# Retention, routed experts and a channel mix in one kernel: where the last two row blocks of wv are narrowed

## The chip, the cores and the metric

One core of a Trainium2 chip runs the whole program. The metric is the device time of one execution in microseconds (us). Before the change the median of three runs is 459.07 us.

## The reference, cut to what matters

Three layers follow one another on 2 x 768 tokens of width 512:

```python
x = retention(q, k, v, lam)                   # 8 heads of 64, blocks of 64
e = expert_of_each_token(x, w_gate, w_local)  # one expert of 8, in order of the sequence
y = p[e] * (relu(x @ w1[e]) @ w2[e])          # w1: 512 x 1024, w2: 1024 x 512
x_prev = shift(y, 1)
xk = mu_k * y + (1 - mu_k) * x_prev
xr = mu_r * y + (1 - mu_r) * x_prev
k = relu(xk @ w_k)                            # w_k: 512 x 1024
out = sigmoid(xr @ w_r) * ((k * k) @ w_v)     # w_r: 512 x 512, w_v: 1024 x 512
```

The last layer is the channel mix. Its three weights w_k, w_v and w_r are float64 and reach the kernel as 64-bit words, so they have to be turned into float32 ("narrowed") on the chip.

## The kernel before, in words

Every product is made in three matmuls of a rounded format (fp32r): each operand is split into a high part (a cast on ScalarE, ACT) and a low part (source minus high, on VectorE, DVE), and high x high, high x low and low x high are summed in PSUM (`split3`, L652, and `k_high` and `k_low` in the mix). Each engine works through its instructions in the order in which the program writes them.

*The experts* run one after another (`up`, L659, and `down`, L699), 256 token slots each. `up` makes four pieces of the hidden layer; for each, PE runs 24 matmuls into a PSUM tile `ps_h` (three such tiles), ACT writes the high part `hh` (L669) and DVE the low part `hl` (L670), after which the PSUM tile is free for the piece after the next two. `down` uses the four pieces in order. Within `up` and `down` the function `side_w` is called 8 times an expert, 64 times in all, counted here from 0. A call splits one or two staged weight pieces (`w_split`: cast L155, subtraction L156, and on the SP queue the load of the piece four further on) and takes `ns` steps of the narrowing.

*The narrowing* (`narrow`, L754) takes one 128 x 512 part in three steps of DVE work: `narrow_1` (L743, L744), `narrow_2` (L747, L748) and `narrow_3` (L751, L752). ACT has the magnitude of the next part (L739) at the end of the third step; the load of the part after the next (L767, 512 KB) is issued there too. The parts are 8 of wk, 4 of wr and 8 of wv. The first 18 are written back to DRAM by the SP queue (L788) and later loaded and split like any other weight. The last two, row blocks 6 and 7 of wv, aren't written: `divide` (L795) makes their two parts of `w2` at once. That makes 60 steps behind a first one that only loads. From call 4 to call 51 a call takes one step, and two where its number leaves 5 when divided by 8 (calls 5, 13, 21, 29, 37, 45); calls 52 to 54 take two each, and `divide` comes in calls 57 and 59.

*The channel mix* takes six groups of 256 tokens. The order of the program is k_begin and k_part for group 0, r_part 0, k_part 1, mix(1, 1), and then in turn v_part of one group, r_part of the next and k_part of the one after. `k_part` (L1042) makes four pieces; for each PE runs its matmuls into `ps_k`, ACT applies Relu into `rl` (L1064) and Square into `kh` (L1065), DVE makes `sq = rl * rl` (L1067) and the low part (L1068), and then `after(fp)` runs whatever is put there. For group 0 that is `first_k`: mix_first behind piece 0, `weigh(1)` (ACT, L995) behind piece 1, and behind piece 3 the transposes of group 1 (`fetch`), `mix(1, 0)` (DVE L906 and L915, ACT L902 and L914) and a read. `k_part` 1 needs `mix(1, 0)`. `v_part` (L1083) takes the eight row blocks of wv in order, three matmuls each (L655 to L657): high, low, high part of the block's weights.

Of the kernel before, what the change touches and what calls it, by code (L numbers as in the profile page):

```python
# [10 lines left out]
F32 = mybir.dt.float32  # L11
# [3 lines left out]
I32 = mybir.dt.int32  # L15
AF = mybir.ActivationFunctionType
ALU = mybir.AluOpType
# [4 lines left out]
P = 128  # L22
B, H, S, D = 2, 8, 768, 64
DM = H * D
NE, FF = 8, 1024
# [5 lines left out]
NF = FF // P  # L31
# [13 lines left out]
def kernel(  # L45
# [16 lines left out]
    act, dve, pool, pe, sp = nc.scalar, nc.vector, nc.gpsimd, nc.tensor, nc.sync  # L62
# [48 lines left out]
    NV = NF - 2  # L111
    wk32 = dp.tile([P, ND, FF], F32, name="wk32")
    wr32 = dp.tile([P, ND, DM], F32, name="wr32")
    wv32 = dp.tile([P, NV, DM], F32, name="wv32")
# [8 lines left out]
    W = {}  # L123
# [20 lines left out]
    def w_split(k=1, eng=dve):  # L144
        for _ in range(k):
            if at[1] >= len(pieces):
                return
            while at[0] <= at[1]:
                w_load()
            kind, i, src, n, f, j, m = pieces[at[1]]  # L150
            if (kind, i) not in W:
                W[kind, i] = w_tiles(kind, i, n, f)
            hi, lo = W[kind, i]
            t = staged.pop(at[1])
            act.copy(out=hi[:, j : j + m, :], in_=t)  # L155
            eng.tensor_tensor(out=lo[:, j : j + m, :], in0=t, in1=hi[:, j : j + m, :].bitcast(F32), op=ALU.subtract)  # L156
            at[1] += 1
            w_load()
# [21 lines left out]
    with ExitStack() as actx:  # L180
# [54 lines left out]
        for h in range(H):  # L235
            dve.tensor_tensor_scan(
                out=msk[:, h % 2, h // 2, :], data0=lams[:, h : h + 1].to_broadcast([P, P]), data1=ident, initial=0.0, op0=ALU.mult, op1=ALU.add
# [395 lines left out]
    with ExitStack() as bctx:  # L633
# [87 lines left out]
        ys, written = [], []  # L721
# [9 lines left out]
        def words(raw):  # L731
            return (
                raw.bitcast(mybir.dt.uint32).rearrange("p (n t) -> p n t", t=2)[:, :, 0],
                raw.bitcast(I32).rearrange("p (n t) -> p n t", t=2)[:, :, 1],
                raw.bitcast(F32).rearrange("p (n t) -> p n t", t=2)[:, :, 1],
            )

        def magnitude(raw, t):
            act.activation(out=t.bitcast(F32), in_=words(raw)[2], func=AF.Abs)  # L739

        def narrow_1(t):

            dve.tensor_scalar(out=t.bitcast(F32), in0=t.bitcast(F32), scalar1=2.0**-15, scalar2=TOP64, op0=ALU.max, op1=ALU.min)  # L743
            dve.tensor_scalar(out=t, in0=t, scalar1=3, scalar2=0x3FFFFFFF, op0=ALU.logical_shift_left, op1=ALU.bitwise_and)  # L744

        def narrow_2(raw, t, t2, p2):
            dve.scalar_tensor_tensor(out=t2, in0=words(raw)[1], scalar=-(1 << 30), in1=t, op0=ALU.bitwise_and, op1=ALU.bitwise_or)  # L747
            dve.tensor_scalar(out=p2, in0=t2, scalar1=-(1 << 23), scalar2=None, op0=ALU.bitwise_and)  # L748

        def narrow_3(raw, p2, low, t2, x):  # L750
            dve.scalar_tensor_tensor(out=low, in0=words(raw)[0], scalar=2.0**-52, in1=p2, op0=ALU.mult, op1=ALU.mult)  # L751
            dve.tensor_tensor(out=x, in0=low, in1=t2.bitcast(F32), op=ALU.add)  # L752

        def narrow():  # L754

            n = DM
            parts = []
            for src, dst in ((wk, wk32), (wr, wr32), (wv, wv32)):
                sv, dv = (x.rearrange("p a b -> p (a b)") for x in (src, dst))
                parts += [(sv[:, j : j + n], dv[:, j : j + n]) for j in range(0, dv.shape[1], n)]  # L760
            parts += [(wv[:, j, :], j) for j in range(NV, NF)]
            raws, ts = {}, {}

            def read(k):
                if k < len(parts):
                    raws[k] = bp.tile([P, n], mybir.dt.int64, name=f"raw64_{k}", tag="raw64")
                    sp.dma_start(out=raws[k], in_=parts[k][0])  # L767

            def begin(k):
                if k < len(parts):  # L770
                    ts[k] = tp.tile([P, n], I32, name="t1", tag="t1")
                    magnitude(raws[k], ts[k])

            read(0)
            read(1)
            yield
            begin(0)
            for k in range(len(parts)):
                t2 = tp.tile([P, n], I32, name="t2", tag="t2", bufs=3)
                narrow_1(ts[k])  # L780
                yield
                narrow_2(raws[k], ts[k], t2, ts[k])
                yield
                narrow_3(raws[k], ts[k].bitcast(F32), ts[k].bitcast(F32), t2, t2.bitcast(F32))
                if isinstance(parts[k][1], int):
                    whole.append((parts[k][1], t2.bitcast(F32)))
                else:
                    written.append(lambda t=t2, k=k: sp.dma_start(out=parts[k][1], in_=t.bitcast(F32)))  # L788
                begin(k + 1)
                read(k + 2)  # L790
                yield

        whole = []

        def divide():  # L795

            j, x = whole.pop(0)
            hi, lo = (w[:, j, :] for w in W["w2", NE])
            act.copy(out=hi, in_=x)
            dve.tensor_tensor(out=lo, in0=x, in1=hi.bitcast(F32), op=ALU.subtract)  # L800

        conv = narrow()
        perm = bp.tile([P, 2, 2 * P], F32R, name="perm", bufs=1)
# [128 lines left out]
        def side_w():  # L932
            c = calls[0]
            calls[0] += 1
            late = list(written)

            ws, ns, vs = 1, 1, 0
            if c < 4:
                ws, ns = (2, 2, 1, 1)[c], c == 2
            elif c >= 52:  # L940
                ws, ns, vs = ((1, 2, 0), (1, 2, 0), (1, 2, 0), (1, 0, 0), (1, 0, 0), (1, 0, 1), (1, 0, 0), (0, 0, 1), (1, 0, 0), (1, 0, 0), (0, 0, 0), (0, 0, 0))[c - 52]
            elif c % 8 == 5:
                ns = 2
            w_split(ws)
            for _ in range(ns):
                next(conv, None)
            for _ in range(vs):
                divide()
            for w in late:
                w()  # L950
            del written[: len(late)]
# [15 lines left out]
    with ExitStack() as mctx:  # L967
        mp = mctx.enter_context(tc.tile_pool(name="mp", bufs=2))
# [3 lines left out]
        GS = 2 * P  # L972
# [11 lines left out]
        def read(n):  # L984
            if n < NN:
                xgs[n] = xsp.tile([P, 2, DM], F32, name=f"xg{n}", tag="xs")
                for i in range(2):
                    u = unit(n, i)
                    sp.dma_start(out=xgs[n][:, i, :], in_=Y_n[u * P : (u + 1) * P, :])

        def weigh(n):
            if n < NN:
                for i in range(2):
                    u, x = unit(n, i), xgs[n][:, i, :]
                    act.activation(out=x, in_=x, func=AF.Copy, scale=pe_p[:, u : u + 1])  # L995
# [56 lines left out]
        def k_part(n, xk, pk, after):  # L1052

            k2[n] = []
            for fp in range(NF // 2):
                ds = (2, 3) if fp in pk else range(ND)
                if fp not in pk:
                    pk[fp] = psk.tile([P, 2, GS], F32, name=f"ps_k{n}{fp}", tag="k")
                ps = pk[fp]
                k_high(ps, fp, ds, xk)  # L1060
                k_low(ps, fp, ds, xk)
                rl = mp.tile([P, 2, GS], F32, name="rl", tag="rl")
                kh, kl = (mp.tile([P, 2, GS], F32R, name=f"k2{x}{n}{fp}", tag=f"k2{x}", bufs=NF) for x in "hl")
                act.activation(out=rl, in_=ps, func=AF.Relu)  # L1064
                act.activation(out=kh, in_=rl, func=AF.Square)  # L1065
                sq = mp.tile([P, 2, GS], F32, name="sq", tag="sq")
                dve.tensor_tensor(out=sq, in0=rl, in1=rl, op=ALU.mult)  # L1067
                dve.tensor_tensor(out=kl, in0=sq, in1=kh.bitcast(F32), op=ALU.subtract)  # L1068
                k2[n].append((kh, kl))
                after(fp)  # L1070

# [11 lines left out]
        def v_part(n, after):  # L1083
            b, g = todo[n]
            for t in range(2):
# [10 lines left out]
                    sp.dma_start(out=out[b, g * GS + t * P : g * GS + (t + 1) * P, w], in_=o[:, w])  # L1096
                after(t)

        def none(_):
            pass  # L1100

        def first_k(fp):
            if fp == 0:
                mix_first(1, 1)
                x_new(1)
                for a in range(2):
                    act.copy(out=xt[1][:, 2 * a : 2 * a + 2, 0:1], in_=px[1 + a][:, :, GS - 1 : GS])
            if fp == 1:
                weigh(1)
            if fp == NF // 2 - 1:  # L1110
                fetch(1)
                xk[1] = mix(1, 0)
                read(2)


        xk, xr = {0: x0[0]}, {}
# [2 lines left out]
        xr[0] = x0[1]  # L1119
        k_part(0, xk[0], pk, first_k)  # L1120
        r_part(0, xr[0])
        k_part(1, xk[1], {}, lambda fp: fp == 1 and weigh(2))
        xr[1] = mix(1, 1)
        for n in range(1, NN):

# [61 lines left out]
```

## Time and profile before

| what | value |
| --- | --- |
| runs of the kernel before | 459.07 us median (458.91, 459.07, 461.42) |
| the profiled execution's own time | 458.06 us |
| its span, first to last instruction | 456.4 us |
| PE busy | 436.7 us (96%) |
| DVE busy | 309.9 us (68%) |
| ACT busy | 229.2 us (50%) |
| mean granted TensorE clock | 0.993 |

The span runs from the first instruction to the last; some 1.7 us of the execution's time lie around it. Matmuls are pipelined, so PE's busy time says that PE had work in flight, not how much of its peak it gave. In the profile PE stands for TensorE's matmuls, DVE for VectorE, ACT for ScalarE, and SPq for the DMA queue of SyncE. An idle time in brackets is that of the engine just before the instruction, with what ended it.

### The profile page before, as it was taken

What the parts mean: (1) busy time and instruction counts of PE and PEld (TensorE: products, weight loads), DVE (VectorE), ACT (ScalarE), POOL (GpSimd) and SP (SyncE); (2) the same over time, 40 slices, a digit from 0 to 9 for tenths busy, and PEclk for the clock granted to TensorE, in tenths of its full rate; (3) what the DMA queues carried; (4) which work ended last, traced back from release to release, by engine and by line L of the source; (5) the groups of instructions that cost most, each with busy time, mean ns of one, the idle gap of its engine ahead of it and who ended that gap; (6) DMA issues with size and microseconds to landing.
All of it is one profiled execution on the core that took longest, in us unless ns stands there. A gap on an engine that the chain in (4) does not pass through costs nothing.

```text
span 456.4 us, 8308 instructions
## 1 busy us (share of the span) xinstructions
PE 436.7 (96%) x3243; PEld 391.3 (86%) x3243; DVE 309.9 (68%) x602; ACT 229.2 (50%) x386; POOL 65.6 (14%) x92
## 2 busy tenths in 40 slices
PE   6999988999798999999999999999999999999996
PEld 4888776979688898989898999998898988989886
DVE  6678875775989899998989995746255262552501
ACT  2455532565475465747465653866255462653410
POOL 3433323500312021232110101000000000000000
PEclk9999998999998999999999999999999999999999
DMA  7999934497979999999989741201102002010001
GB/s 254 341 382 341 412 124 139 147 315 259 323 244 324 322 312 355 293 366 302 335 303 311 242 144 43 93 1 34 60 1 92 1 25 68 0 47 1 12 36 47
DMA packets 29111, 85.03 MB, mean 186 GB/s; under 512 B 4351, under 2 KB 5131, under 8 KB 29068
## 3 DMA queue, kind: packets, MB, share of 16 engines
q1 hardware_dynamic: 25004, 73.45, 47.1%
q0 software_dynamic: 2624, 8.39, 5.1%
q10 hardware_dynamic: 1440, 2.62, 1.5%
q8 instruction: 26, 0.43, 0.4%
q14 instruction: 17, 0.14, 0.1%
HBM read 68.71 MB, written 15.74 MB: 185 GB/s over the span
## 4 chain that ended last, share of the span: by engine, by line
PE 69%; DVE 13%; DMA 8%; ACT 4%; issue 4%; POOL 1%; SPq 1%; DVEq 0%; ACTq 0%; POOLq 0%
PE ps_y L655 5%; PE ps_y L657 5%; PE ps_y L656 5%; PE ps_v L655 5%; PE ps_v L656 5%; PE ps_v L657 5%; PE ps_h L655 5%; PE ps_h L656 5%; PE ps_h L657 5%; PE ps_k L1028 4%; PE ps_k L1029 4%; PE ps_k L1035 4%; DMA raw<-in_w_dram 4%; DVE w1l L156 2%; PE ps_r L655 2%
## 5 line engine op out<-in xcount | busy, mean ns | idle before, releaser
L655 PE MATMUL ps_h<-xsTh,w1h 128*128 128x256 f32 x256 | 73.6, 288 | 4.4 <-DVE hl L670 4.4
L656 PE MATMUL ps_h<-xsTl,w1h 128*128 128x256 f32 x256 | 73.4, 287 | 0.1
L657 PE MATMUL ps_h<-xsTh,w1l 128*128 128x256 f32 x256 | 73.0, 285 | 0.0
L1067 DVE TENSOR_TENSOR sq<-rl 128x512 f32<-128x512 f32 x24 | 16.6, 692 | 56.3 <-ACT rl L1064 56.3
L655 PEld LDWEIGHTS ps_h<-xsTh,w1h 128*128 128x128 f32 x256 | 49.7, 194 | 5.4 <-DVE hl L670 4.8
L655 PE MATMUL ps_y<-w2h,hh 128*128 128x512 f32 (+1 forms) x136 | 52.6, 387 | 0.0
L657 PE MATMUL ps_y<-w2h,hl 128*128 128x512 f32 (+1 forms) x136 | 51.9, 382 | 0.0
L656 PE MATMUL ps_y<-w2l,hh 128*128 128x512 f32 (+1 forms) x136 | 51.9, 382 | 0.0
L656 PEld LDWEIGHTS ps_h<-xsTl,w1h 128*128 128x128 f32 x256 | 49.8, 195 | 0.9 <-DVE xsTl L174 0.5
L156 DVE TENSOR_TENSOR w1l<-raw,w1h 128x1024 fp32r<-128x1024 f32 x38 | 46.3, 1220 | 5.3 <-ACT w1h L155 4.9
L657 PEld LDWEIGHTS ps_h<-xsTh,w1l 128*128 128x128 f32 x256 | 49.8, 195 | 0.0
L156 DVE TENSOR_TENSOR w2l<-raw,w2h 128x1024 fp32r<-128x1024 f32 x35 | 42.6, 1216 | 3.7 <-ACT w2h L155 3.5
L739 ACT ACTIVATE t<-raw 128x512 f32<-128x512 f32 x20 | 13.5, 677 | 55.8 <-DMA raw<-in_wk_dram 24.4
L155 ACT CAST w1h<-raw 128x1024 fp32r<-128x1024 f32 x38 | 38.7, 1052 | 3.5 <-DMA raw<-in_w_dram 3.0
L155 ACT CAST w2h<-raw 128x1024 fp32r<-128x1024 f32 x35 | 36.7, 1048 | 6.0 <-DMA raw<-in_w_dram 4.9
L655 PE MATMUL ps_v<-w2h,k2h 128*128 128x512 f32 (+1 forms) x104 | 39.2, 377 | 0.0
L656 PE MATMUL ps_v<-w2l,k2h 128*128 128x512 f32 (+1 forms) x104 | 38.8, 373 | 0.0
L657 PE MATMUL ps_v<-w2h,k2l 128*128 128x512 f32 (+1 forms) x104 | 38.8, 373 | 0.0
L726 POOL DMA_INDIRECT Y_n<-y,sidx x16 | 17.9, 1118 | 144.1 <-ACT y L716 81.3
L657 PEld LDWEIGHTS ps_y<-w2h,hl 128*128 128x128 f32 x136 | 25.6, 188 | 5.5 <-DVE hl L670 0.2
L656 PEld LDWEIGHTS ps_y<-w2l,hh 128*128 128x128 f32 x136 | 25.6, 188 | 5.1
L655 PEld LDWEIGHTS ps_y<-w2h,hh 128*128 128x128 f32 x136 | 25.6, 188 | 5.1
(210 smaller groups left out, 964.4 us busy)
## 6 DMA issues: line engine op xcount, KB each, us to landing
raw<-in_w_dram SPq DMA_DIRECT2D x64, 512.0 KB
kv<-in_kv_dram SPq DMA_DIRECT2D x12, 512.0 KB
qk<-in_qk_dram SPq DMA_DIRECT2D x11, 512.0 KB
raw<-in_wk_dram SPq DMA_DIRECT2D x8, 512.0 KB
raw<-in_wv_dram SPq DMA_DIRECT2D x8, 512.0 KB
out_dram<-o SPq DMA_DIRECT2D x11, 256.0 KB
X_n<-xn ACTq DMA_DIRECT2D x10, 256.0 KB
xg<-Y_n SPq DMA_DIRECT2D x10, 256.0 KB
```

The source lines that it names most:

```text
L155: act.copy(out=hi[:, j : j + m, :], in_=t)
L156: eng.tensor_tensor(out=lo[:, j : j + m, :], in0=t, in1=hi[:, j : j + m, :].bitcast(F32), op=ALU.subtract)
L655: pe.matmul(ps, wh, xh, start=first, stop=False)
L656: pe.matmul(ps, wh, xl, start=False, stop=False)
L657: pe.matmul(ps, wl, xh, start=False, stop=last)
L726: pool.indirect_dma_start(out=Y_n[:, :], out_offset=bass.IndirectOffsetOnAxis(ap=sidx[:, t, e : e + 1], axis=0), in_=y, in_offset=None)
L739: act.activation(out=t.bitcast(F32), in_=words(raw)[2], func=AF.Abs)
L1028: pe.matmul(ps[:, j, :], wkh[:, d, f], x[0][:, d, :], start=j == d == 0, stop=False, skip_group_check=True)
L1029: pe.matmul(ps[:, j, :], wkl[:, d, f], x[0][:, d, :], start=False, stop=False, skip_group_check=True)
L1035: pe.matmul(ps[:, j, :], wkh[:, d, f], x[1][:, d, :], start=False, stop=d == ND - 1, skip_group_check=True)
L1067: dve.tensor_tensor(out=sq, in0=rl, in1=rl, op=ALU.mult)
```

## The change

The two row blocks leave the experts: `narrow` makes 18 parts, in the order wk, wv, wr, and every call from 4 to 51 takes one step; calls 52 to 54 still take two. `divide` goes. In the channel mix a new generator, `last_rows`, loads row block 6, narrows it, splits it, and then does the same for row block 7, in pieces placed by hand between the pieces of k_part 0 and k_part 1. Its tiles take the room of `sq`: the square is now made in place in `rl`.

```diff
-            for src, dst in ((wk, wk32), (wr, wr32), (wv, wv32)):
+            for src, dst in ((wk, wk32), (wv, wv32), (wr, wr32)):
...
-            parts += [(wv[:, j, :], j) for j in range(NV, NF)]
...
-            elif c % 8 == 5:
-                ns = 2
+                ws, ns = int(c not in (59, 62, 63)), 2 if c < 55 else 0
...
-                sq = mp.tile([P, 2, GS], F32, name="sq", tag="sq")
-                dve.tensor_tensor(out=sq, in0=rl, in1=rl, op=ALU.mult)
-                dve.tensor_tensor(out=kl, in0=sq, in1=kh.bitcast(F32), op=ALU.subtract)
+                dve.tensor_tensor(out=rl, in0=rl, in1=rl, op=ALU.mult)
+                dve.tensor_tensor(out=kl, in0=rl, in1=kh.bitcast(F32), op=ALU.subtract)
...
+        def last_rows():
+            def read(j):
+                raw = mp.tile([P, DM], mybir.dt.int64, name=f"r64_{j}", tag="r64", bufs=1)
+                sp.dma_start(out=raw, in_=wv[:, j, :])
+                return raw
+            raw = read(NV)
+            yield
+            for j in range(NV, NF):
+                t, t2 = (mp.tile([P, DM], I32, name=f"{x}c{j}", tag=f"{x}c", bufs=1) for x in ("t1", "t2"))
+                hi, lo = (w[:, j, :] for w in W["w2", NE])
+                magnitude(raw, t)
+                yield
+                narrow_1(t)
+                narrow_2(raw, t, t2, t)
+                yield
+                x = t2.bitcast(F32)
+                narrow_3(raw, t.bitcast(F32), t.bitcast(F32), t2, x)
+                if j + 1 < NF:
+                    raw = read(j + 1)
+                yield
+                act.copy(out=hi, in_=x)
+                dve.tensor_tensor(out=lo, in0=x, in1=hi.bitcast(F32), op=ALU.subtract)
+                yield
...
+            if fp in (1, 2):
+                next(rows)
             if fp == 1:
                 weigh(1)
...
         r_part(0, xr[0])
-        k_part(1, xk[1], {}, lambda fp: fp == 1 and weigh(2))
+        next(rows)
+        def second_k(fp):
+            if fp == 1:
+                weigh(2)
+            if fp != 1:
+                next(rows)
+        k_part(1, xk[1], {}, second_k)
+        next(rows)
+        next(rows)
         xr[1] = mix(1, 1)
```

So block 6 has its load at the start of the channel mix, its magnitude behind piece 1 of k_part 0, its first two steps behind piece 2, its third step behind r_part 0 and its split behind piece 0 of k_part 1. Block 7 has its load behind the third step of block 6, its magnitude behind piece 2 of k_part 1, its first two steps behind piece 3, and its third step and its split between k_part 1 and mix(1, 1).

## Rows read from the trace of the kernel before

**Rows 1.** Windows: length, busy time by engine, then granted clock, DMA share, GB/s.

```profile
114.80:117.30 2.50, 0.00 (x1) 0.00 (x0) 2.46 (x5) 0.93 (x2) 1.23 (x1) 1.00 0.99 324
...
141.10:143.10 2.00, 0.06 (x2) 0.01 (x1) 1.97 (x5) 0.00 (x0) 0.29 (x1) 1.00 0.93 352
...
144.00:147.40 3.40, 3.40 (x18) 3.40 (x17) 3.37 (x6) 3.25 (x5) 1.98 (x2) 0.50 0.92 322
...
299.40:442.00 142.60, 142.60 (x867) 128.11 (x868) 61.57 (x105) 66.63 (x122) 0.49 (x3) 1.00 0.09 30
```

**Rows 2.** Waits of PE from 100 to 160 us: total, times, longest.

```profile
PE ps_h L655 <- DVE hl L670: 4.4, 2, 2.5
```

**Rows 3.** Timeline of PE: k_part 1 waits, and block 7 in v_part 0.

```profile
299.39 0.39 PE L1028 MATMUL ps_k<-w1h,w1h 128*128 128x256 f32 x1 [0.52 <-ACT w1h L914]
...
315.06 0.39 PE L656 MATMUL ps_v<-w2l,k2h 128*128 128x512 f32 x1
```

**Rows 4.** Timeline of DVE in the first three experts: start, duration, instruction.

```profile
113.57 0.42 DVE L743 TENSOR_SCALAR t<-t 128x512 f32<-128x512 f32 x1
...
114.37 1.22 DVE L156 TENSOR_TENSOR w1l<-raw,w1h 128x1024 fp32r<-128x1024 f32 x1
115.50 0.68 DVE L747 SCALAR_TENSOR_TENSOR t<-raw,t 128x512 int32<-128x512 int32 x1
...
116.57 0.68 DVE L670 SCALAR_TENSOR_TENSOR hl<-ps_h,hh 128x512 fp32r<-128x512 f32 x1
...
142.35 0.68 DVE L670 SCALAR_TENSOR_TENSOR hl<-ps_h,hh 128x512 fp32r<-128x512 f32 x1
...
150.80 0.68 DVE L670 SCALAR_TENSOR_TENSOR hl<-ps_h,hh 128x512 fp32r<-128x512 f32 x1
```

**Rows 5.** Timeline of DVE: a third step, a `divide`, and the channel mix's start.

```profile
254.28 0.68 DVE L751 SCALAR_TENSOR_TENSOR t<-raw,t 128x512 f32<-128x512 uint32 x1
...
255.61 0.42 DVE L743 TENSOR_SCALAR t<-t 128x512 f32<-128x512 f32 x1
...
267.78 0.68 DVE L800 TENSOR_TENSOR w2l<-t,w2h 128x512 fp32r<-128x512 f32 x1
...
286.30 0.68 DVE L1067 TENSOR_TENSOR sq<-rl 128x512 f32<-128x512 f32 x1
287.09 0.69 DVE L1068 TENSOR_TENSOR k2l<-sq,k2h 128x512 fp32r<-128x512 f32 x1
287.70 0.87 DVE L906 SCALAR_TENSOR_TENSOR t<-ps_f,mus,t 128x256 f32<-128x256 f32 x2
...
295.63 0.89 DVE L906 SCALAR_TENSOR_TENSOR t<-xt,mus,t 128x256 f32<-128x256 f32 x2 [0.49 <-ACT t L902]
```

**Rows 6.** Timeline of PE: `down` of expert 2, first use of the fourth piece's `hl`.

```profile
153.10 0.40 PE L657 MATMUL ps_y<-w2h,hl 128*128 128x512 f32 x1
```

**Rows 7.** Timeline of ACT: in expert 1, and the channel mix's groups 0 and 1.

```profile
116.37 0.67 ACT L739 ACTIVATE t<-raw 128x512 f32<-128x512 f32 x1 [2.76 <-DMA raw<-in_wk_dram]
116.94 0.58 ACT L669 ACTIVATE hh<-ps_h 128x512 fp32r<-128x512 f32 x1
...
286.20 0.63 ACT L1065 ACTIVATE k2h<-rl 128x512 fp32r<-128x512 f32 x1
...
290.41 1.32 ACT L995 ACTIVATE xg<-xg,pe_p 128x512 f32<-128x512 f32 x2
291.64 0.57 ACT L1064 ACTIVATE rl<-ps_k 128x512 f32<-128x512 f32 x1
...
310.24 0.60 ACT L1064 ACTIVATE rl<-ps_k 128x512 f32<-128x512 f32 x1 [1.62 <-PE ps_k L1035]
```

**Rows 8.** The ACT cast of a `divide`, in the timeline of ACT.

```profile
266.27 0.62 ACT L799 CAST w2h<-t 128x512 fp32r<-128x512 f32 x1
```

**Rows 9.** Timeline of the SP queue: the reads of groups 1 and 2.

```profile
284.52 1.74 SPq L989 DMA_DIRECT2D xg<-Y_n  x4
```

**Rows 10.** The chain that ended last: the load of a raw part.

```profile
99.04 8.06 DMA raw<-in_wk_dram
```

More of the change, by code (lines that the diff above doesn't have):

```diff
@@ L784, in narrow @@
                 narrow_3(raws[k], ts[k].bitcast(F32), ts[k].bitcast(F32), t2, t2.bitcast(F32))
[L785 to L788, printed above, removed]
+                written.append(lambda t=t2, k=k: sp.dma_start(out=parts[k][1], in_=t.bitcast(F32)))
                 begin(k + 1)
@@ L791, in narrow @@
                 yield
[L793 to L800, printed above, removed]
         conv = narrow()
@@ L935, in side_w @@
             late = list(written)
-            ws, ns, vs = 1, 1, 0
+            ws, ns = 1, 1
             if c < 4:
@@ L940, in side_w @@
             elif c >= 52:
-                ws, ns, vs = ((1, 2, 0), (1, 2, 0), (1, 2, 0), (1, 0, 0), (1, 0, 0), (1, 0, 1), (1, 0, 0), (0, 0, 1), (1, 0, 0), (1, 0, 0), (0, 0, 0), (0, 0, 0))[c - 52]
-            elif c % 8 == 5:
-                ns = 2
+                ws, ns = int(c not in (59, 62, 63)), 2 if c < 55 else 0
             w_split(ws)
@@ L946, in side_w @@
                 next(conv, None)
-            for _ in range(vs):
-                divide()
             for w in late:
@@ L1097, in v_part @@
                 after(t)
+        def last_rows():
[21 more added lines that the diff above has]
+                yield
+        rows = last_rows()
+        next(rows)
         def none(_):
@@ L1121 @@
         r_part(0, xr[0])
-        k_part(1, xk[1], {}, lambda fp: fp == 1 and weigh(2))
+        next(rows)
[6 more added lines that the diff above has]
+        next(rows)
+        next(rows)
         xr[1] = mix(1, 1)
```

## The prediction, made before the changed kernel was run

> **What bounds the kernel now.** I read first the windows by stage, then who waited for whom on PE, then the timelines of the engines around each wait. From 299.4 us to 442 us PE is busy in every microsecond while DVE works 62 of 143 us [rows 1]: from there on, work for DVE or ACT costs nothing unless a matmul comes to wait for it. Up to there PE waits in three places that concern the change. Two are in the first experts: PE asks for a free `ps_h` and DVE hasn't yet written the `hl` that frees it, 4.4 us in two waits, the longer 2.5 us [rows 2]. The windows show that DVE is busy through both (2.46 of 2.50 us, 1.97 of 2.00 us), so it is behind with its queue and not waiting itself [rows 1]. Behind the second the granted clock is 0.50 for 3.4 us, the lower level of 1.2 GHz; behind the first it stays at 1.00 [rows 1]. The third is 0.52 us at k_part 1, where PE waits for ACT's cast in mix(1, 0) [rows 3].
>
> **What the experts gain.** The narrowing's unit prices are read as distances from one start to the next. A first step is 113.57 to 114.37, 0.80 us; a second step is 115.50 to 116.57, 1.07 us [rows 4]; a third is 254.28 to 255.61, 1.33 us [rows 5]. Of the six steps that go, two lie before the second wait's end (calls 5 and 13). Counted from call 4 to call 15, the steps on DVE ahead of the `hl` at 142.35 are five first, five second and four third ones before, and four of each after. So one first and one second step go, 0.80 + 1.07 = 1.87 us. Since DVE is behind in this stretch, PE is let go that much earlier. I take **-1.9 us**. Bounds: nothing, if the loads of raw words set the pace and not DVE; at most 4.4 us, both waits.
>
> With 1.87 us less, the two waits shrink to some 1.4 and 1.1 us, and I expect no low clock behind them: the row that shows none is the one behind 2.5 us, so the length alone doesn't decide, but less idle time speaks for less. The low clock's 3.4 us at half speed did 1.7 us of full-speed work [rows 1], so that much is to be had. What could be late next is the `hl` of the fourth piece of expert 2: `down` first reads it at 153.10 [rows 6], and DVE has it at 150.80 + 0.68 = 151.5 [rows 4]. After the change PE would come 1.87 and 1.7 us earlier, at 149.5, and DVE 1.9 us earlier, at 149.6: 0.1 us is given back, and I take **-1.6 us** (bounds -1.7 and 0).
>
> The other four removed steps and the two `divide` lie where PE doesn't wait; I cost them at nothing. The same holds for the order wk, wv, wr: the last part of wr is written one call ahead of its load, and should that load be late, its user, r_part 0, comes only behind the whole of k_part 0.
>
> **What the channel mix pays, first place: mix(1, 0).** In k_part 0 ACT and DVE go hand in hand towards the 0.52 us wait, so additions count. First, the square in place may not be written before ACT's Square has read `rl`: Square ends at 286.20 + 0.63 = 286.83 [rows 7], where the product began at 286.30 [rows 5], +0.57 us, handed on through mix_first to ACT. Second, the magnitude of block 6 stands ahead of weigh(1): 116.37 to 116.94 is 0.57 us [rows 7]. So ACT's Relu of piece 2 moves from 291.64 [rows 7] by 1.14 to 292.78, and its Square ends at about 294.02. From there DVE has, in its order: product of piece 2 at 294.05, 0.79 us later the low part, 0.61 us later the narrowing (both distances from 286.30, 287.09 and 287.70 [rows 5]), that is from 295.45; first and second step, 1.87 us, to 297.32; product and low part of piece 3, 1.40 us, to 298.72. Then mix(1, 0) begins, which before began at 295.63 [rows 5]. That is 3.1 us later, and the chain from there to PE's 299.39 [rows 3] keeps its length: **+3.1 us**. PE spends it in pieces of 1.0 to 1.5 us: at the transposes behind weigh(1), before k_part 1 and inside it. Bounds: 1.1 us, if DVE had room for the narrowing and only ACT's chain counted; 3.7 us with another 0.57.
>
> **Second place: block 7 in v_part 0.** Its split comes last, and v_part 0 follows k_part 1 at once. Measured from the Relu of piece 3 at 310.24 [rows 7], on the clock of before: Relu 0.60 and Square 0.63 us end at 311.5; product and low part 1.40 us, to 312.94; first and second step 1.87 us, to 314.81; third step 1.33 us, whose last result stands at about 316.2; cast of 0.62 us [rows 8] to 316.86; subtraction of 0.68 us [rows 5] to 317.6. PE reaches the first matmul that reads block 7's low part at 315.06 [rows 3]. So it waits **+2.5 us** in all, for the cast first and then for the subtraction. The eight blocks are taken in order and nothing else of v_part can be run in between. Bounds: 2.0 us if only the cast's wait counted, 3.3 us if the cast stood behind another ACT operation of 0.6 us.
>
> Mix(1, 1) starts some 5 us later than before, but r_part 1 needs it only after v_part 0, whose 48 matmuls and 8 transposes cover it: no cost. In later groups the product moves by 0.6 us, under a PE that is always busy: no cost.
>
> **The DMAs that move.** Two loads of 512 KB leave the middle of the experts, with no write. Block 6's now stands on the SP queue ahead of the four reads at 284.52 [rows 9]; its room comes free with the last matmuls that read the experts' tiles, and those reads wait for the experts' last rows anyway. If that cover fails, the reads and weigh(1) are late by as much. Block 7's load is issued once block 6's third step has read the words, behind mix(1, 0), at about 304 (299.39 and 3.1, then a subtraction and L751); the longest such load took 8.06 us [rows 10], which makes 312. Its magnitude stands just ahead of the Relu at 310.24 + 3.1 = 313.3 [rows 7], so it costs nothing, at most 0.4 us. POOL's queue isn't passed.
>
> **The clock.** Of the two long waits of before one was followed by 1.7 us of loss. The second place's wait is as long as they are, so it gets half, **+0.85 us** (bounds 0 and 1.7). The first place's comes in shorter pieces with matmuls between, nearest to the 0.52 us one behind which the window from 299.4 shows a clock of 1.00 [rows 1, 3]: nothing, at most 1.7 us.
>
> **Sum:** -1.9 - 1.6 + 3.1 + 2.5 + 0.85 = +2.95 us. Against the profiled execution's 458.06 us that is 461.0 us. That execution is 1.0 us below the median of the runs, and the difference is set on the median, 459.07: **462.0 us**, slower by 0.6%. A measurement of this kernel can tell about 0.5% (2.3 us) from no change.
>
> **Rivals.**
> *Both new waits bring the low clock* (chance 0.13). PE then pays 0.85 us more in v_part 0 and 1.7 us in k_part 1: 464.6 us. For it: the low clock came behind 1.9 us of idle time. Against it: not behind 2.5 us. The Trainium skill, "TensorE: Matmul & The Clock Gate", section "A second HAM failure mode: psum-queue depth-cycling", says that frequent small idle spells between groups of matmuls make the clock fall and rise again, with a price each time. By that rule this rival would be the likeliest; the trace agrees in one of its two waits.
> *The raw loads set the pace of the early experts* (0.07). Then the gains, 3.5 us, are missing: 465.5 us. For it: ACT waits 2.76 us for a raw part at 116.37 [rows 7]. Against it: DVE is busy through both waits.
> *DVE has room in k_part 0* (0.16). Only ACT's 1.1 us counts in the first place: 459.07 + 2.95 - 2.0 = 460.0 us, no change. For it: DVE waited 0.49 us before mix(1, 0) [rows 5]. Against it: that is a fifth of what comes in.
> *The backlog in the experts dissolves* (0.07), the other side. A shorter queue lets DVE catch up early, so that both waits (4.4 us) and the low clock (1.7 us) go, 6.1 us; it decides once the two new waits stay under 3.8 us together. With their lower bounds, 1.1 and 2.0, the time is 456.1 us. Against it: only 1.87 us of work leave the queue ahead of 142.35.
>
> **How the numbers follow.** The forecast has 0.57, with a range of its own from 460.5 to 464.2 (no low clock in v_part 0 and a little less in both places; a whole one and a little more); about 0.11 of it lies under 461.4, the border of slower by 0.5%. Slower: 0.46 + 0.13 + 0.07 = 0.66. Within 0.5%: 0.11 + 0.16 = 0.27. Faster: 0.07. The range from 459.0 to 465.5 leaves out the rival on the faster side and what lies beyond the two upper rivals.
>
> **What would show it.** In the changed profile: PE's two waits for `hl` near 116 and 141 us at some 1.4 and 1.1 us, with a clock of 1.00 behind them; a wait of PE at k_part 1 for ACT's cast in mix(1, 0), in pieces that sum to 2 us or more; a wait of PE in v_part 0 for the last row's cast or subtraction of 2 to 3 us. Wrong would be: DVE with idle time between piece 2 and mix(1, 0), no wait in v_part 0, or waits in the experts that stay as they were.

## The result, and the profile after

The changed kernel takes 463.15 us (median of 12 runs, 461.63 to 465.08), the kernel before 458.99 us beside it (median of 12, 456.89 to 461.55). The ratio is 1.0089 with a 95% interval from 1.0065 to 1.0113: slower by 0.9%, or 4.2 us, where 2.95 us were forecast; 463.15 lies in the range given, 459.0 to 465.5. In all that follows, a ratio leaves out the runs more than 1.5% above the fastest of their kernel, and a median takes in all runs. The profiled execution of the changed kernel (called after from here on) took 462.94 us.

The first view is the list of what PE waited for from 95 to 456 us, as total, times and longest; it answers to [rows 2, 3].

```profile
PE ps_k L1011 <- ACT w1h L901: 2.2, 2, 1.2
PE ps_v L655 <- ACT w2h L1104: 2.1, 1, 2.1
PE ps_h L655 <- DVE hl L670: 2.1, 2, 1.4
PE ps_t L996 <- ACT xg L978: 1.0, 1, 1.0
PE ps_x L649 <- DMA xs<-X_n,gidx: 0.7, 1, 0.7
PE ps_v L656 <- DVE w2l L1105: 0.2, 1, 0.2
```

The waits for `hl` in the experts are 2.1 us where they were 4.4. New are 1.0 us at the transposes, 2.2 us at k_part 1 (0.5 before), both on the way through mix(1, 0), and 2.3 us in v_part 0 for the cast and the subtraction of block 7. The timeline of PE gives the place of each:

```profile
116.29 0.38 PE L655 MATMUL ps_h<-xsTh,w1h 128*128 128x256 f32 x1 [0.65 <-DVE hl L670]
...
141.55 0.39 PE L655 MATMUL ps_h<-xsTh,w1h 128*128 128x256 f32 x1 [1.44 <-DVE hl L670]
...
289.49 1.27 PE L996 MATMUL ps_t<-ident,xg 128*128 128x128 f32 x8 [1.00 <-ACT xg L978]
...
297.46 0.39 PE L1011 MATMUL ps_k<-w1h,w1h 128*128 128x256 f32 x1 [1.23 <-ACT w1h L901]
...
299.63 0.39 PE L1011 MATMUL ps_k<-w1h,w1h 128*128 128x256 f32 x1 [0.95 <-ACT w1h L901]
...
317.33 0.50 PE L655 MATMUL ps_v<-w2h,k2h 128*128 128x512 f32 x1 [2.10 <-ACT w2h L1104]
...
318.06 0.79 PE L656 MATMUL ps_v<-w2l,k2h 128*128 128x512 f32 x1 [0.22 <-DVE w2l L1105]
```

A list of waits doesn't say what a stretch costs. For that the span is cut at four events that both kernels have: DVE's first narrowing step (the first instruction of L743), the first matmul into `ps_k`, the ninth matmul of k_part 1 (behind the last wait for mix(1, 0)), and DVE's last product `o`. Two rows of the timeline of before that don't stand above, the first `ps_k` and the last `o`:

```profile
279.09 0.28 PE L1028 MATMUL ps_k<-xkh,w1h 128*128 128x256 f32 x1
...
452.81 0.42 DVE L1095 TENSOR_TENSOR o<-ps_v,sg 128x256 f32<-128x256 f32 x1 [2.40 <-PE ps_v L657]
```

and the same two of after:

```profile
276.36 0.28 PE L1011 MATMUL ps_k<-xkh,w1h 128*128 128x256 f32 x1
...
457.57 0.42 DVE L1077 TENSOR_TENSOR o<-ps_v,sg 128x256 f32<-128x256 f32 x1 [2.40 <-PE ps_v L657]
```

The first L743 starts at 107.83 before and 108.02 after; the ninth matmul is at 299.39 [rows 3] and 299.63. So:

| stretch | before | after | difference | forecast |
| --- | --- | --- | --- | --- |
| A: L743 to first `ps_k` (experts) | 171.26 | 168.34 | -2.92 | -3.5 |
| B: to ninth matmul of k_part 1 (mix(1, 0)) | 20.30 | 23.27 | +2.97 | +3.1 |
| C: to last `o` (v_part 0 and the rest) | 153.42 | 157.94 | +4.52 | +3.35 |

The three differences sum to 4.57 us; with the 0.19 us by which after reaches its first L743 later, that is 4.76 us. Each sign is as forecast; what is missing is 1.2 us in C and 0.6 us in A.

The windows, with columns as in [rows 1], show the clock behind each wait:

```profile
142.00:150.00 8.00, 8.00 (x51) 6.97 (x49) 7.90 (x12) 6.06 (x10) 2.84 (x2) 1.00 0.97 356
...
299.60:304.00 4.40, 4.37 (x36) 4.37 (x37) 2.82 (x5) 2.70 (x5) 0.00 (x0) 1.00 0.40 121
...
318.00:321.40 3.40, 3.34 (x12) 2.95 (x13) 2.27 (x6) 1.92 (x5) 0.11 (x1) 0.50 0.00 0
...
321.40:324.00 2.60, 2.60 (x13) 2.13 (x12) 2.07 (x4) 2.10 (x5) 0.00 (x0) 0.99 0.10 32
```

The low clock in expert 2 [rows 1] is gone, and behind the waits at k_part 1 there is none. Behind the wait in v_part 0 it is 0.50, the lower level, for 3.4 us, which is 1.7 us of full-speed work: as much as the low clock in the experts had cost before.

How the work of block 7 reaches v_part 0 is read in the timeline of DVE, and then in the cast of ACT:

```profile
312.50 0.69 DVE L1050 TENSOR_TENSOR k2l<-rl,k2h 128x512 fp32r<-128x512 f32 x1
313.11 0.42 DVE L743 TENSOR_SCALAR t1c<-t1c 128x512 f32<-128x512 f32 x1
...
315.94 0.69 DVE L752 TENSOR_TENSOR t2c<-t1c,t2c 128x512 f32<-128x512 f32 x1
...
317.31 0.69 DVE L1105 TENSOR_TENSOR w2l<-t2c,w2h 128x512 fp32r<-128x512 f32 x1 [0.68 <-ACT w2h L1104]
```

```profile
316.66 0.62 ACT L1104 CAST w2h<-t2c 128x512 fp32r<-128x512 f32 x1 [4.92 <-DVE t2c L752]
```

From the last low part of k_part 1 on, DVE does nothing but block 7, without a gap up to the cast, and ACT stands idle for 4.92 us until the third step is done. PE takes the cast at 317.33, 0.05 us after it ends (316.66 + 0.62).

### The profile page after: what moved, and what is told of

Its sections match the earlier page's. It is cut to its first block, busy times and chain, and to the rows that moved or that the text cites. A ratio compares the mean times of both kernels' runs of the same rounds, so it can differ in the third digit from the quotient of the medians.

```text
span 461.2 us, 8291 instructions
## 1 busy us (share of the span) xinstructions
PE 441.0 (96%) x3243; PEld 393.0 (85%) x3243; DVE 310.7 (67%) x602; ACT 229.2 (50%) x386; POOL 67.6 (15%) x92
## 4 chain that ended last, share of the span: by engine, by line
PE 60%; DVE 10%; ACT 4%; DMA 4%; issue 2%; SPq 0%; DVEq 0%; ACTq 0%
PE ps_y L657 5%; PE ps_v L656 5%; PE ps_y L655 5%; PE ps_y L656 5%; PE ps_v L657 4%; PE ps_v L655 4%; PE ps_k L1011 4%; PE ps_k L1012 4%; PE ps_k L1018 4%; PE ps_h L656 4%; PE ps_h L657 4%; PE ps_h L655 4%; DMA raw<-in_wk_dram 3%; DVE w2l L156 2%; PE ps_r L655 2%
## 5 line engine op out<-in xcount | busy, mean ns | idle before, releaser
L1049 DVE TENSOR_TENSOR rl<-rl 128x512 f32<-128x512 f32 x24 | 16.6, 692 | 58.9 <-ACT k2h L1048 58.9
L726 POOL DMA_INDIRECT Y_n<-y,sidx x16 | 19.4, 1215 | 140.4 <-ACT y L716 76.2
L739 ACT ACTIVATE t<-raw 128x512 f32<-128x512 f32 x18 | 12.2, 677 | 35.3 <-DMA raw<-in_wk_dram 18.1
```

The costliest lines, as they stand in the source:

```text
L726: pool.indirect_dma_start(out=Y_n[:, :], out_offset=bass.IndirectOffsetOnAxis(ap=sidx[:, t, e : e + 1], axis=0), in_=y, in_offset=None)
L1049: dve.tensor_tensor(out=rl, in0=rl, in1=rl, op=ALU.mult)
```

## The experiments

All were compared with the kernel before on the same chip; ratios are to it, with 95% intervals (none for a single run). A, B and C are the stretches above, each worked out from rows of the timeline of that kernel's profile.

### The square in place, alone (e2_square_in_place)

In the kernel before:

```diff
-                sq = mp.tile([P, 2, GS], F32, name="sq", tag="sq")
-                dve.tensor_tensor(out=sq, in0=rl, in1=rl, op=ALU.mult)
-                dve.tensor_tensor(out=kl, in0=sq, in1=kh.bitcast(F32), op=ALU.subtract)
+                dve.tensor_tensor(out=rl, in0=rl, in1=rl, op=ALU.mult)
+                dve.tensor_tensor(out=kl, in0=rl, in1=kh.bitcast(F32), op=ALU.subtract)
```

> The kernel before with the square made in place in rl, nothing else. Theory: ACT's Square of piece 0 now holds DVE's product by 0.6 us, and this runs through to mix(1, 0): PE's wait at k_part 1 grows from 0.5 to some 1.1 us, or part of it shows at the transposes before it; the rest of the kernel is unchanged, some 0.5 us in all. Rival (the in-place square is what makes the changed kernel slow): waits of 2 us or more in the channel mix. Rival (it costs nothing): 0.5 us as before.

Measured: one run of 461.03 us, whose experts A took 173.37 us, 2.1 more than before's, in a part that the edit doesn't touch: there the clock is low behind both early waits of PE, where in before it is low behind the second alone.

```profile
119.00:122.40 3.40, 3.40 (x18) 3.40 (x18) 3.33 (x6) 2.01 (x4) 1.57 (x2) 0.51 0.81 275
146.30:149.70 3.40, 3.40 (x18) 3.40 (x17) 3.33 (x6) 2.08 (x4) 0.65 (x1) 0.51 0.96 342
```

So only the stretch counts: B is 20.81 us, +0.51. PE's timeline shows where:

```profile
294.13 1.27 PE L1013 MATMUL ps_t<-ident,xg 128*128 128x128 f32 x8 [0.44 <-ACT xg L995]
...
302.36 0.38 PE L1028 MATMUL ps_k<-w1h,w1h 128*128 128x256 f32 x1 [0.53 <-ACT w1h L914]
```

The wait at k_part 1 stays as it was, and a new one of 0.44 us comes at the transposes, whose `xg` ACT weighs behind mix_first. The delay that the product hands on to ACT was put at 0.57 us; the rows of the prediction give 286.83 - 286.30 = 0.53, and B has 0.51.

### The steps of block 6 behind mix(1, 0) (e4_steps_behind_mix)

In the changed kernel, the first and second step of block 6 go behind r_part 0:

```diff
-            if fp in (1, 2):
+            if fp == 1:
                 next(rows)
...
         next(rows)
+        next(rows)
```

> The changed kernel, with the first two steps of block 6 moved from behind piece 2 of k_part 0 to behind r_part 0, that is behind mix(1, 0) on DVE. Theory (DVE's 1.9 us of steps sit ahead of mix(1, 0)): the wait for the cast at k_part 1 shrinks by 1.8 us to some 0.4 us, beside the 1.0 us at the transposes, which stays since the magnitude is not moved; time 1.8 us below the changed kernel, about 461.3 us; v_part 0 and its half clock unchanged. Rival (ACT's chain alone sets mix(1, 0), by the magnitude and the square in place): no change, 463 us.

Measured: 460.29 us, ratio 1.003 (0.9995 to 1.0064). B is 21.36 us, 1.91 less than after's. The rows of PE's timeline, to be held against those of after:

```profile
290.69 1.27 PE L996 MATMUL ps_t<-ident,xg 128*128 128x128 f32 x8 [1.00 <-ACT xg L978]
...
298.91 0.39 PE L1011 MATMUL ps_k<-w1h,w1h 128*128 128x256 f32 x1 [0.53 <-ACT w1h L901]
...
316.63 0.60 PE L655 MATMUL ps_v<-w2h,k2h 128*128 128x512 f32 x1 [2.11 <-ACT w2h L1104]
```

At k_part 1 PE is back at one wait of 0.53 us. The two steps were priced at 1.87 us on DVE and cost PE 1.91: DVE had no room for them in k_part 0, and the rival that gave it room falls. The wait in v_part 0 isn't touched, and neither is the low clock behind it (windows: 0.72 for 316 to 318 us, 0.62 for 318 to 321, together 1.7 us of full-speed work lost). The medians of after and e4 are 2.9 us apart, more than that. The runs' mean granted clock, 0.994 on average in e4 and 0.991 in after, speaks for about one low clock less in a run of e4; that is an estimate, as only one execution of each has a trace.

### The square in a tile of its own (e6_square_apart)

In the changed kernel, the square is again made in a tile beside `rl`, of which there is one:

```diff
-                dve.tensor_tensor(out=rl, in0=rl, in1=rl, op=ALU.mult)
-                dve.tensor_tensor(out=kl, in0=rl, in1=kh.bitcast(F32), op=ALU.subtract)
+                sq = mp.tile([P, 2, GS], F32, name="sq", tag="sq", bufs=1)
+                dve.tensor_tensor(out=sq, in0=rl, in1=rl, op=ALU.mult)
+                dve.tensor_tensor(out=kl, in0=sq, in1=kh.bitcast(F32), op=ALU.subtract)
```

> The changed kernel with the square in a tile of its own again (one buffer), nothing else. Theory: the product no longer waits for ACT's Square, so mix(1, 0) begins some 1.1 us earlier; the three waits of PE around k_part 1, 3.2 us together, shrink to some 2 us; the wait in v_part 0 shrinks by at most 0.6 us, from 2.3 to 1.7 us; time about 461.5 us, still above the kernel before. Rival (the square in place is the whole cost): 459 us.

Measured: 461.03 us, ratio 1.0063 (1.0032 to 1.0095). B is 22.24 us, 1.03 less than after's, and C 157.34, 0.60 less: PE's wait in v_part 0 for the cast is 1.5 us in place of 2.1. So the in-place square also stood in the chain to v_part 0, by 0.6 us. The low clock is there in e6 too (0.57 from 317 to 321 us). In B the square costs twice what e2 showed. DVE's timeline shows the second half at piece 2; first e6, then after:

```profile
289.77 0.69 DVE L1050 TENSOR_TENSOR sq<-rl 128x512 f32<-128x512 f32 x1 [1.46 <-ACT rl L1047]
```

```profile
291.23 0.69 DVE L1049 TENSOR_TENSOR rl<-rl 128x512 f32<-128x512 f32 x1 [1.51 <-ACT k2h L1048]
```

In e6 the product starts when Relu ends, in after only when Square ends, some 0.7 us further on. Before, DVE had 0.49 us free ahead of mix(1, 0) [rows 5] to take that up, so e2 doesn't show it; with block 6's steps in between it has none.

### Block 7 back in the experts (e3_block7_in_experts)

In the changed kernel, block 7 is again the last part of `narrow`, and its split stands in call 59:

```diff
+            parts.append((wv[:, NF - 1, :], NF - 1))
...
+            elif c in (29, 37, 45):
+                ns = 2
...
+            if c == 59:
+                divide()
...
-            for j in range(NV, NF):
+            for j in range(NV, NF - 1):
```

> The changed kernel, with row block 7 narrowed and split in the experts again (three extra steps at calls 29, 37, 45, its split at call 59) and only block 6 left in the channel mix. Theory (the tail of block 7 costs PE's wait of 2.3 us in v_part 0 and 1.7 us of half clock behind it): no wait of PE for the last row in v_part 0, clock 1.00 there, the wait at k_part 1 unchanged at some 3 us with the transposes, time 4 us below the changed kernel, about 459 us. Rival (the clock falls for another reason): only the 2.3 us go, about 461 us. Rival (in v_part 0 something else is late next): a new wait there, time as the changed kernel.

Measured: 458.37 us, ratio 1.0014 (0.9982 to 1.0046). v_part 0 has no wait, and C is 154.85 us, 3.09 less than after's. A stays at 168.50: three more steps in the later experts cost nothing that shows. But C is still 1.43 us above that of before, and windows of e3 show why:

```profile
300.00:303.50 3.50, 3.50 (x20) 3.50 (x20) 1.61 (x3) 0.79 (x3) 0.00 (x0) 0.58 0.02 5
...
310.00:320.00 10.00, 10.00 (x57) 8.66 (x56) 6.47 (x12) 6.04 (x13) 0.11 (x1) 1.00 0.00 1
```

The low clock is now behind k_part 1, 0.58 for 3.5 us, which is 1.5 us lost. Its two waits there are 1.23 and 0.95 us, as in after, where the clock behind them was 1.00. The profiled execution has a mean granted clock of 0.991, and nine of the twelve runs have 0.995 or more, so most of them seem to have had one low clock less. The two waits in PE's timeline:

```profile
297.48 0.38 PE L1028 MATMUL ps_k<-w1h,w1h 128*128 128x256 f32 x1 [1.23 <-ACT w1h L914]
...
299.65 0.58 PE L1028 MATMUL ps_k<-w1h,w1h 128*128 128x256 f32 x1 [0.95 <-ACT w1h L914]
```

### The row work where DVE has room (e5_rows_in_gaps)

In the changed kernel, nothing of the two blocks stands in k_part 0 any more. Block 6's magnitude and three steps go behind r_part 0, its split behind piece 0 of k_part 1; block 7 has its magnitude and first two steps behind piece 1, ahead of weigh(2), and its third step and its split behind piece 2, one piece earlier than the end:

```diff
-            if fp in (1, 2):
-                next(rows)
...
-        next(rows)
+        for _ in range(3):
+            next(rows)
...
         def second_k(fp):
+            for _ in range((1, 2, 2, 0)[fp]):
+                next(rows)
             if fp == 1:
                 weigh(2)
-            if fp != 1:
-                next(rows)
...
-        next(rows)
-        next(rows)
```

> The changed kernel, with the work on both row blocks moved: magnitude and all three steps of block 6 behind r_part 0; in k_part 1 the split of block 6 behind piece 0, magnitude and first two steps of block 7 behind piece 1, third step and split behind piece 2. Theory: DVE has some 1.4 us free in each piece of k_part 1, so both waits go: at k_part 1 only the square in place is left (0.6 us above the 0.5 us of before), in v_part 0 nothing, no half clock there; time 463.15 - 2.4 - 2.3 - 1.7, about 456.7 us, below the kernel before by 2 us. Rival (the pieces of k_part 1 have no room): PE waits there for ps_k, or the wait in v_part 0 stays at 1 us or more, time 459 us or more.

Measured: 455.60 us, ratio 0.9935 (0.9905 to 0.9966), faster than both kernels, by 0.65% against the kernel before. The profiled execution, of 458.45 us, reached its first L743 only at 110.74 us; its stretches are A 168.23, B 20.81 and C 153.43. The waits of PE that are left in the channel mix:

```profile
291.56 1.27 PE L996 MATMUL ps_t<-ident,xg 128*128 128x128 f32 x8 [0.45 <-ACT xg L978]
...
299.78 0.39 PE L1011 MATMUL ps_k<-w1h,w1h 128*128 128x256 f32 x1 [0.53 <-ACT w1h L901]
```

and the window behind them:

```profile
300.00:320.00 20.00, 20.00 (x135) 18.43 (x135) 16.01 (x28) 11.54 (x22) 0.11 (x1) 1.00 0.09 28
```

All of DVE's work on the two blocks is in these 20 us (from 301.30 to 314.83 us), and PE is busy throughout at a clock of 1.00. DVE works 16.0 of the 20 us. What costs 7.5 us in B and C of after (2.97 + 4.52) costs 0.5 here, which is the in-place square's by e2.

### The same, with the square apart (e8_gaps_and_square_apart)

The edit of e5 with that of e6.

> The kernel of e5 (both row blocks in the gaps of k_part 1) with the square in a tile of its own again. Theory: the 0.4 us wait at the transposes goes and mix(1, 0) is as before, so 0.5 us below e5, about 455.1 us, less than the runs can tell from e5; in the profile no wait at the transposes and 0.5 us at k_part 1. Rival (the square in place wasn't on the path in e5): the same waits as in e5.

Measured: 456.04 us, ratio 0.9944 (0.9918 to 0.9970). By the runs it can't be told from e5. In the trace B is 20.28 us, 0.53 less than e5's and that of before to 0.02, and C is 153.44. With e4 and e5, B of after comes apart: 23.27 to 21.36 by the steps (1.91), to 20.81 by the magnitude (0.55), to 20.28 by the square (0.53), 2.99 in all. The shares depend on the order in which the parts are taken off: with the steps still in place the square alone was 1.03 (e6).

### The experts: the same steps in other calls (e1_steps_later, e7_steps_in_down, e10_all_in_experts)

These three begin from the kernel before and keep all 60 steps in the experts. They ask whether the gain in A needs the two blocks to leave, or only fewer steps early.

```diff
-            elif c % 8 == 5:
+            elif c in (21, 29, 33, 37, 41, 45):
                 ns = 2
```

> The kernel before with one edit: the second narrowing steps of calls 5 and 13 move to calls 33 and 41 neighbours (21, 29, 33, 37, 41, 45 take two). Everything else, block 6 and 7 of wv included, stays in the experts. Theory (DVE's queue in the first two experts sets PE's waits for hl): the two waits together fall from 4.4 us to some 2.1 us, as in the changed kernel, the low clock behind the second goes, and the time is 1.9 to 3.5 us below the kernel before, about 456 us. Rival (the loads of raw words set the pace): the waits stay near 4.4 us and the time within 1 us of the kernel before. Rival (the later calls have no room either): new waits of PE behind 150 us, time not below before.

Measured: 463.02 us (six runs, one of them of 1480 us), ratio 1.0107 (1.0051 to 1.0163). A is 175.10 us, 3.8 more than before's: PE waits for `hl` seven times, five in `up` and two in `down`:

```profile
PE ps_h L655 <- DVE hl L670: 4.6, 5, 1.4
PE ps_y L657 <- DVE hl L670: 1.6, 2, 0.9
```

The expected gain didn't come; the early waits shrank and others came at 167 to 228 us.

```diff
-            elif c % 8 == 5:
+            elif c in (21, 23, 29, 37, 45, 47):
                 ns = 2
```

> The kernel before with calls 21, 23, 29, 37, 45 and 47 taking two steps instead of 5, 13, 21, 29, 37, 45, so all second steps lie in the down half of an expert. In e1, two of the moved steps lay in the up half, where ACT's wait for the raw words of the next part stands in front of the hh that PE needs. Theory (it was their place in up): few waits behind 150 us, the two early waits as in e1, time 1 to 3 us below the kernel before. Rival (the experts' loads and DVE have no room for the steps once PE runs ahead): waits for hl behind 150 us of 3 us or more together, time as the kernel before or above it.

Measured: 461.53 us, ratio 1.0036 (0.9997 to 1.0074), A 174.71. The timeline of ACT shows what a double step does to its loads:

```profile
168.38 0.68 ACT L739 ACTIVATE t<-raw 128x512 f32<-128x512 f32 x1 [6.20 <-DMA raw<-in_wk_dram]
...
169.43 0.60 ACT L669 ACTIVATE hh<-ps_h 128x512 fp32r<-128x512 f32 x1
```

and the chain that ended last passes through that load:

```profile
160.63 7.67 DMA raw<-in_wk_dram
```

The load is issued at 160.63 and lands 7.67 us later; the magnitude that needs it stands on ACT ahead of an `hh`, so ACT, DVE's `hl` and PE behind them wait for a DMA:

```profile
170.81 0.38 PE L655 MATMUL ps_h<-xsTh,w1h 128*128 128x256 f32 x1 [1.79 <-DVE hl L670]
```

Counted in the schedule, three calls lie from a load to its magnitude, and two where a double step comes between. In the kernel before, the magnitudes with two calls all stand in call 5 of an expert from call 13 on; in e7 they stand in calls 23, 25, 30, 38, 46, 48 and 53. The magnitude at 168.38 is that of call 23, the last of its expert, with the next expert's first `hh` behind it. In the changed kernel there are three calls for every magnitude from call 9 to 51.

```diff
-            for src, dst in ((wk, wk32), (wr, wr32), (wv, wv32)):
+            for src, dst in ((wk, wk32), (wv, wv32), (wr, wr32)):
...
+                ws, vs = int(c not in (59, 62, 63)), int(c in (59, 61))
+                ns = 2 if c < 55 else int(c < 58)
...
-            elif c % 8 == 5:
+            elif c in (29, 37, 45):
                 ns = 2
```

> The kernel before, with the parts in the order wk, wv, wr, second steps only in calls 29, 37 and 45 (those of 5, 13 and 21 come at the end, one each in calls 55, 56, 57) and the two splits in calls 59 and 61; the channel mix is untouched, the square is in its own tile. In e1 and e7 the load of a raw part had only two calls instead of three before ACT's magnitude stood waiting for it, and several of these fell in the up half; here, as in the kernel before, those with two calls fall in call 5 of an expert only, where no hh waits behind. Theory (distance from load to use, not lack of room, made e1 and e7 slow): the early waits as in the changed kernel, some 1 to 2 us, no low clock behind them, no waits from 150 us on, time 2 to 3.5 us below the kernel before, about 456 us. Rival (no room for 60 steps once PE runs ahead): waits for hl behind 150 us as in e7, time 458.5 us or more.

Measured: 459.58 us, ratio 0.9976 (0.9947 to 1.0005), A 171.79. In the middle, the magnitudes two calls behind their load again stand in call 5 of an expert (29, 37, 45), in the midst of `down`, and no matmul of PE waits for an `hl` from 150 to 250 us. The granted clock is 1.00 over all of A, where the kernel before has its low clock of 3.4 us. But the steps that were put off come back at the end, in the timeline of PE:

```profile
265.89 0.39 PE L655 MATMUL ps_h<-xsTh,w1h 128*128 128x256 f32 x1 [1.96 <-DVE hl L670]
...
278.93 0.38 PE L881 MATMUL ps_f<-perm,yll 128*128 128x256 f32 x1 [1.03 <-DVE yll L875]
```

DVE is busy for 92.8 of the 100 us from 150 to 250:

```profile
150.00:250.00 100.00, 99.96 (x633) 89.88 (x632) 92.82 (x134) 58.20 (x82) 17.10 (x16) 1.00 0.93 321
```

So DVE has hardly any room in the experts: A is 171.26 in the kernel before and 171.79 to 175.10 in these three, and 168.2 to 169.1 in the five made from the changed kernel, from whose experts steps have left. In e3, three of the six steps are enough. The profiled executions of e7 and e10 took 464.33 and 463.04 us, 2.8 and 3.5 above their medians; their first L743 comes 2.8 and 4.3 us later than in before's profile, which is outside A. None of the three placements with all 60 steps in the experts made A shorter than 171.26. That steps had to leave is shown for these placements only; others, and a third buffer for the raw words, which would have given the loads more time, weren't tried.

## Why the prediction was right, and where it was short

**The experts, forecast -3.5, measured -2.92.** The queue term is right: from the first L743 to the `hl` that PE waits for second is 142.35 - 107.83 = 34.52 us before [rows 4], and 140.80 - 108.02 = 32.78 after, so -1.74 where -1.87 was worked out. The two waits were put at 1.4 and 1.1 us and are 0.65 and 1.44, 2.1 in all in place of 2.5. The start of that `hl` after, and of the next one that `down` reads:

```profile
140.80 0.69 DVE L670 SCALAR_TENSOR_TENSOR hl<-ps_h,hh 128x512 fp32r<-128x512 f32 x1 [0.34 <-ACT hh L669]
...
149.53 0.68 DVE L670 SCALAR_TENSOR_TENSOR hl<-ps_h,hh 128x512 fp32r<-128x512 f32 x1
```

Ahead of the first of them DVE itself waits 0.34 us for ACT's `hh`: the backlog is used up there, which may be why the full 1.87 didn't come.

The mis-sized term is the clock: -1.6 was forecast and 2.92 - 1.74 = 1.18 came. The low clock did go. Two steps of that term were off, and the 24th matmul from the second wait, where the low clock of before has ended, tells them apart (before, then after):

```profile
147.45 0.28 PE L657 MATMUL ps_h<-xsTh,w1l 128*128 128x256 f32 x1
```

```profile
144.40 0.28 PE L657 MATMUL ps_h<-xsTh,w1l 128*128 128x256 f32 x1
```

Counted from the first L743 it starts at 39.62 before and 36.38 after, 3.24 earlier, of which 1.73 were there when the wait ended. So the low clock was worth 1.5 us here and not the 1.7 of "3.4 us at half speed". The other step is "0.1 us is given back" in `down`: DVE took 8.73 us between these two `hl`, where it had taken 8.45 [rows 4], and PE had to wait for its weights:

```profile
150.26 0.19 PEld L657 LDWEIGHTS ps_y<-w2h,hl 128*128 128x128 f32 x1 [0.49 <-DVE hl L670]
```

A PE that isn't slowed down reaches the next thing that DVE has late. The matmul that uses these weights starts at 150.27, where it started at 153.10 before [rows 6], so 0.22 us are given back there, and 0.10 more at the matmul behind it (150.60 and 153.33): 3.24 - 0.32 = 2.92.

All of this is one execution of each kernel, and A varies: with the experts of before it is 171.26 and 173.37 (before, e2), mostly by the low clocks in it, and with those of after 168.23 to 169.13 (after, e4, e5, e6, e8). The two groups don't overlap, so there is a gain; but the 0.6 us by which it fell short of the forecast is no more than what A varies by.

**mix(1, 0), forecast +3.1, measured +2.97.** Its three parts were put at 0.57 (square), 0.57 (magnitude) and 1.87 (steps), and the runs e8, e5 and e4 give 0.53, 0.55 and 1.91, taken off in the order steps, magnitude, square. The method, adding up DVE's queue instruction by instruction from the Relu of piece 2, held; so did the division into pieces of some 1 us and the clock that stays at 1.00, though e3 shows that this needn't be.

**v_part 0, forecast +3.35, measured +4.52.** The wait was put at 2.5 us and is listed as 2.10 + 0.22. The step that failed is "so it gets half, +0.85 us": the low clock came whole, 1.7 us, and it came in all three profiles with a wait of that kind (after, e4 and e6). It isn't certain, though: of e4's twelve runs the fastest (456.49 us) has a mean granted clock of 1.000, so in it the clock fell nowhere. Half of an event that comes whole or not at all is a mean over two cases and belongs to neither of them.

The listed waits leave out 0.44 us, and the starts of the matmuls show where they are. In v_part 0 one matmul starts some 0.23 us behind the other and lasts 0.39, so it overlaps the next; a wait is counted only from its end. The first two matmuls of block 7 start 2.26 and 0.50 us later than they would have behind the one before them, 2.76 us in all: the +2.5 us of the forecast was 0.26 short. At the third matmul of v_part 0's second token tile the low clock has ended (before, then after):

```profile
315.28 0.40 PE L657 MATMUL ps_v<-w2h,k2l 128*128 128x512 f32 x1
...
316.86 0.39 PE L657 MATMUL ps_v<-w2h,k2l 128*128 128x512 f32 x1
```

```profile
321.56 0.40 PE L657 MATMUL ps_v<-w2h,k2l 128*128 128x512 f32 x1
```

It starts 4.70 us later than before, where the matmul at 318.06 started 3.00 later (315.06 before [rows 3]): 1.70 us for the low clock. With 2.76 that is 4.46 of the 4.52.

**The pieces at no cost** held. The load of block 7 was issued at 300.97 and its magnitude didn't wait; mix(1, 1) made PE wait nowhere; neither did the reads behind block 6's load.

**The rivals.** That DVE has room in k_part 0 falls by e4. That the backlog in the experts dissolves falls: 2.1 us of waits stayed. That the raw loads set the pace of the early experts falls for after, whose A shrank, but e7 shows a kernel in which they do. The rival with the low clock in both new waits is half of what happened in v_part 0; after shows none at k_part 1. The Trainium skill, "TensorE: Matmul & The Clock Gate", section "A second HAM failure mode: psum-queue depth-cycling", says of another kernel that small and frequent idle spells between groups of matmuls made the clock fall and rise again at a cost. The spells here that are nearest to that, the two at k_part 1, agree with it in e3 and not in after; the fall in v_part 0 came behind one long wait and a short one.

## What to carry to other kernels

Moving work off an engine that is full (DVE at 93 of 100 us in the experts) gained here only where it landed in a place with room on that engine: two row blocks cost 7.5 us ahead of mix(1, 0) and v_part 0, the square in place and a low clock included, and 0.5 us one or two pieces away, among 20 us in which DVE works 16 at most. Before such a move, list for each place the next matmul that waits for the engine and what stands between. Between the issue of a load and the instruction that waits for it, count the work in between at its shortest, since everything behind that instruction on its engine waits for the DMA too, as the `hh` behind the magnitude in e7 did.

## What was not expected of the hardware

The same pair of waits, 1.23 and 0.95 us at k_part 1, was followed by a clock of 1.00 in after and of 0.58 for 3.5 us in e3; before, 2.50 us of waiting was followed by 1.00 and the shorter wait by 0.50 [rows 1, 2]. The length of a wait didn't decide in these profiles; what does stays open. Nor is it the kernel alone: with the experts of before, the clock fell behind one early wait in before's profile and behind both in e2's. Each of these low clocks lasts some 3.4 us at half speed, a loss of 1.7 us by the granted clock or 0.0037 of the span, and the mean granted clocks of the twelve runs of e4 go from 0.989 to 1.000. By that estimate one kernel has three low clocks in one run and none in another, and that is one reason why its runs differ.

The first narrowing step, which comes behind the retention layer, lies at 107.83 us in before's profile, 108.02 in after's and 110.74 in e5's, though no edit touches what is ahead of it. The clock has a part in it: in e5's profile it is low (0.51) from 75.0 to 82.0 and from 99.0 to 102.5 us, in before's once, from 75.5 to 79.5. The spread is more than the in-place square costs, and it is why small effects were read from stretches of one trace and not from whole times.
